# Four times twelve token blocks: 10 x 512 + 2 x 480 against 11 x 512 + 448

## The chip, the cores and the metric

The kernel runs on one core of one Trainium2 chip. The metric is the device time of one execution in microseconds (us); shown are the median of several executions and, for the profile, one execution recorded by the hardware profiler.

## The reference

Channel attention, followed by a feed-forward layer with a squared ReLU, all in float32. There are B = 4 batches of N = 6080 tokens with C = 256 channels.

```python
qn = q / (np.linalg.norm(q, axis=1, keepdims=True) + 1e-06)
kn = k / (np.linalg.norm(k, axis=1, keepdims=True) + 1e-06)
s = kn.transpose(0, 2, 1) @ qn / tau          # C x C for each batch
a = softmax(s)                                # over the last axis
x = (v @ a).reshape(B * N, C)
h = np.maximum(x @ w_in, 0.0)                 # w_in: 256 x 2048
out = h * h @ w_out                           # w_out: 2048 x 256
```

## The kernel before, in words

The softmax matrix is folded into the first weight: for each batch W = a @ w_in is made once, so a token block needs two products, v @ W with its squared ReLU, and the product with w_out. Each float32 operand is split into a high and a low part in a rounded format (called fp32r in the rows), and each product is the sum of three matmuls, high-high, high-low and low-high.

The tokens of a batch are cut into `NB` = 12 blocks (lines 75 to 78). `T` = 512 is the widest. Lines 76 and 77 give ten blocks of 512 and divide what is left, 960, into two of 480.

The first two blocks of batch 0 are worked plainly, with 512-column matmuls (`first_product`, `eight_products`). All other blocks are worked as `groups` (line 959): four groups for each block, one for every 512 of the 2048 hidden channels, 46 x 4 = 184 groups. In a group, both products are done by a seven-product scheme for 2 x 2 blocks. For it a token block is cut into two halves of `half_of(k)` columns: 256 for a block of 512, 240 for one of 480. Every matmul of a group has a 128 x 128 stationary operand of its own and `half` moving columns.

```python
987  def product(k, ps, form, block, start=False):
990      half = half_of(k)
992      for p in range(2):
994          w_hi, w_lo = (WF[k, late, i][:, p, at, :] for i in range(2))
995          for i, (wt, vt) in enumerate(((w_hi, v_hi), (w_hi, v_lo), (w_lo, v_hi))):
996              tensor.matmul(ps[:, p, :half], wt, vt[:, block, :], ...)
```

That is six matmuls for a product, and seven products for a group: 42. The second half of the work, `to_output` (lines 1031 to 1049), has 42 more in all but six early groups of batch 0 (`window_A`: three windows of 6, `window_S`: four of 6). A group is thus 84 matmuls.

The order of the work is written out by hand in `PERIOD` (lines 1268 to 1319) and kept on each engine (`InProgramOrder`). A period k issues the products of group k and, beside them, the later steps of groups k - 1 and k - 2:

```python
1269  (0, first_B),       1273  (0, copy_C),
1281  (0, second_C),      1293  (0, third_C),
1298  (0, add_C),         1305  (1, window_A1),
1308  (0, fourth_C),      1312  (1, lambda k: lo_S(k, "S1")),
```

`copy_C` is a ScalarE copy from one PSUM bank to another, onto which `second_C` adds. `add_C` is a VectorE addition with ReLU that reads what `third_C` has summed, before `fourth_C` adds to it. ScalarE squares, copies and makes the high parts; VectorE adds and makes the low parts (`A_lo`, `s_lo`, `v_lo`). SP's queue loads v (`load_v_blocks`) and the forms of W (`load_forms`, 1.8 MB for a group whatever the block's width); POOL's queue sums and stores the outputs (`combine`). In the rows the tiles ps_b, ps_h and ps_c take the products, ps_o the second half, v_hi and v_lo are the parts of v, wf the forms of W, and A, s, wo and wS the parts of the second half.

At the named points of a period (the strings "act", "dve", "sq", "pe", "norms", "mid") pieces of the next batch's attention are issued: `Gram` (12 extra matmuls in a period), the norms (`ps_n`, eight matmuls with one column), the transposes (`ps_t`) and the next weights (`ps_w`, six matmuls of 512 columns). They are counted by periods and not by tokens.

The last group of all is finished without the next period's matmuls beside it (lines 1469 to 1538): its last parts go into ps_end, two VectorE additions make end_o from it, and SP's queue stores that.

Of the kernel before, what the change touches and what calls it, by code (L numbers as in the profile page):

```python
# [32 lines left out]
def kernel(  # L33
# [27 lines left out]
    B, N, C = q.shape  # L61
# [3 lines left out]
    T = 512  # L65
# [7 lines left out]


    NB = -(-N // T)
    left = N - T * max(NB - 2, 0)
    sizes = [T] * (NB - 2) + [left // 2, left - left // 2]
    blocks = [(sum(sizes[:i]), n) for i, n in enumerate(sizes)]
    SPB = NB * NF

# [1488 lines left out]
```

## Time and profile before

| | |
|---|---|
| median of 3 runs | 2097.33 us (2096.82 to 2097.7) |
| the profiled execution's own time | 2098.59 us |
| its span, first to last instruction | 2096.8 us |
| matmuls, each with a weight load | 17158 |
| TensorE busy | 2091.1 us |
| VectorE, ScalarE busy | 1903.4 us, 1890.6 us |
| moved by DMA | 549.78 MB, 262 GB/s on average |

The profiled execution's time is 1.8 us above its span. A busy TensorE is no proof that it works at its peak, because matmuls are pipelined and a record overlaps the next one's. What counts for it is the time from one matmul's start to the next one's start: a stretch's length divided by the matmuls begun in it.

### The profile page before, as it was taken

The page shows a single profiled execution, that of the slowest core. Times are in us where ns is not written, and L with a number is a line of the kernel's source. Part 1 is how long each engine was busy: PE and PEld are TensorE (multiplying, and loading weights), DVE is VectorE, ACT ScalarE, POOL GpSimd, SP SyncE. Part 2 cuts the span into 40 slices and gives each one's busy share as a digit, 9 for nine tenths or more (in the row PEclk, how much of TensorE's full clock was granted, in tenths as well). Part 3 has the DMA queues.
Part 4 walks back from the last instruction along what each step waited for, and adds up shares of the span by engine and source line. Part 5 has one row for each costly group of instructions (what it writes and reads, how often), then busy time and mean ns, then how long its engine had stood idle before and what let it go on. Part 6 is the DMA issues. An engine that isn't in the chain of part 4 may idle for free.

```text
span 2096.8 us, 43463 instructions
## 1 busy us (share of the span) xinstructions
PE 2091.1 (100%) x17158; PEld 2053.8 (98%) x17158; DVE 1903.4 (91%) x2195; ACT 1890.6 (90%) x2379; POOL 350.1 (17%) x430
## 2 busy tenths in 40 slices
PE   9999999999999999999999999999999999999999
PEld 8789999999999999999999999999999999999999
DVE  7898999989999999989998999998999888888887
ACT  5888999889999999989999999998988998998987
POOL 0000111211122111111122111211121121121112
PEclk9999999999999999999999999999999999999999
DMA  9777888789999888789999988877999788787785
GB/s 358 222 224 269 258 255 258 235 261 307 306 279 305 267 262 251 239 243 290 295 294 282 314 252 264 249 244 249 290 284 302 229 244 253 230 248 246 233 245 152
DMA packets 258012, 549.78 MB, mean 262 GB/s; under 512 B 26672, under 2 KB 113072, under 8 KB 257808
## 3 DMA queue, kind: packets, MB, share of 16 engines
q1 hardware_dynamic: 201456, 469.02, 65.7%
q0 software_dynamic: 56352, 77.98, 18.4%
q8 instruction: 135, 2.21, 0.4%
q14 instruction: 69, 0.57, 0.1%
HBM read 433.59 MB, written 58.72 MB: 235 GB/s over the span
## 4 chain that ended last, share of the span: by engine, by line
PE 99%; ACT 1%; DVE 0%; DMA 0%; issue 0%; SPq 0%; DVEq 0%
PE ps_o L29 44%; PE ps_c L29 18%; PE ps_h L29 14%; PE ps_b L29 12%; PE gram L29 7%; PE ps_w L29 2%; ACT x L29 0%; PE ps_end L29 0%; DVE dec L29 0%; DMA qk<-in_q 0%; PE ps_n L29 0%; ACT v_hi L29 0%; ACT s L29 0%; ACT g_hi L29 0%; PE ps_t L29 0%
## 5 line engine op out<-in xcount | busy, mean ns | idle before, releaser
L29 DVE TENSOR_TENSOR x<-x 128x1024 f32<-128x1024 f32 (+2 forms) x549 | 465.3, 848 | 11.1
L29 PE MATMUL ps_c<-v_hi,wf 128*128 128x256 f32 (+1 forms) x2208 | 473.9, 278 | 0.2 <-DVE x L29 0.2
L29 POOL DMA_DIRECT2D o<-o x225 | 232.7, 1188 | 1397.4 <-ACT o L29 899.7
L29 DVE TENSOR_TENSOR s_lo<-x,s_hi 128x1024 fp32r<-128x1024 f32 (+1 forms) x366 | 441.7, 1208 | 16.9 <-ACT s_hi L29 16.5
L29 ACT ACTIVATE x<-x 128x1536 f32<-128x1536 f32 (+4 forms) x384 | 405.0, 1055 | 31.5 <-DVE x L29 29.5
L29 ACT CAST s_hi<-x 128x1024 fp32r<-128x1024 f32 (+1 forms) x366 | 381.8, 1043 | 43.1 <-DVE x L29 42.0
L29 DVE TENSOR_TENSOR A_lo<-x,A_hi 128x1536 fp32r<-128x1536 f32 (+2 forms) x183 | 313.6, 1714 | 81.6 <-ACT A_hi L29 65.3
L29 PEld LDWEIGHTS ps_c<-v_hi,wf 128*128 128x128 f32 x2208 | 375.5, 188 | 1.0 <-DVE x L29 0.4
L29 PE MATMUL ps_h<-v_hi,wf 128*128 128x256 f32 (+1 forms) x1472 | 315.9, 278 | 0.2 <-ACT x L29 0.2
L29 PE MATMUL ps_b<-v_hi,wf 128*128 128x256 f32 (+1 forms) x1472 | 315.8, 278 | 0.0
L29 PE MATMUL ps_c<-v_lo,wf 128*128 128x256 f32 (+1 forms) x1104 | 307.3, 278 | 0.0
L29 ACT CAST A_hi<-x 128x1536 fp32r<-128x1536 f32 (+2 forms) x183 | 264.8, 1447 | 0.0
L29 PEld LDWEIGHTS ps_h<-v_hi,wf 128*128 128x128 f32 x1472 | 250.4, 188 | 0.6 <-ACT x L29 0.6
L29 PEld LDWEIGHTS ps_b<-v_hi,wf 128*128 128x128 f32 x1472 | 250.3, 188 | 0.1
L29 PEld LDWEIGHTS ps_c<-v_lo,wf 128*128 128x128 f32 x1104 | 207.7, 188 | 0.1
L29 PE MATMUL ps_h<-v_lo,wf 128*128 128x256 f32 (+1 forms) x736 | 204.9, 278 | 0.0
L29 PE MATMUL ps_b<-v_lo,wf 128*128 128x256 f32 (+1 forms) x736 | 204.8, 278 | 0.0
L29 PE MATMUL ps_o<-A_hi,wo_hi 128*128 128x256 f32 (+1 forms) x897 | 192.8, 279 | 0.0
L29 PE MATMUL ps_o<-A_hi,wo_lo 128*128 128x256 f32 (+1 forms) x897 | 192.1, 278 | 0.0
L29 PE MATMUL ps_o<-A_lo,wo_hi 128*128 128x256 f32 (+1 forms) x897 | 191.8, 278 | 0.0
L29 PE MATMUL ps_o<-s_hi,wS_lo 128*128 128x256 f32 (+1 forms) x549 | 153.3, 279 | 0.0
L29 PE MATMUL ps_o<-s_lo,wS_hi 128*128 128x256 f32 (+1 forms) x549 | 153.1, 279 | 0.0
(172 smaller groups left out, 5148.9 us busy)
## 6 DMA issues: line engine op xcount, KB each, us to landing
wf<-wf_kept SPq DMA_DIRECT2D x368, 512.0 KB, 5.1
wf<-wf_kept SPq DMA_DIRECT2D x368, 384.0 KB, 4.9
o<-o POOLq DMA_DIRECT2D x114, 256.0 KB, 6.0
qk<-in_k SPq DMA_DIRECT2D x88, 256.0 KB, 5.3
qk<-in_q SPq DMA_DIRECT2D x88, 256.0 KB, 5.4
v<-in_vT SPq DMA_DIRECT2D x76, 256.0 KB, 4.8
out_T<-o POOLq DMA_DIRECT2D x152, 128.0 KB, 5.0
wf_kept<-wS SPq DMA_DIRECT2D x64, 256.0 KB, 6.1
```

The source lines that it names most:

```text
L29: return lambda *args, **kwargs: self.tc.keep_in_program_order(issue(*args, **kwargs))
```

## The change

The twelve blocks of a batch are cut in another way: eleven blocks of 512 tokens and one of 448. `NB`, the groups, the periods and all else stay as they are. Blocks 0 to 9 of each batch are as before; block 10 has 512 tokens (halves of 256 columns) and block 11 has 448 (halves of 224).

```diff
     NB = -(-N // T)
-    left = N - T * max(NB - 2, 0)
-    sizes = [T] * (NB - 2) + [left // 2, left - left // 2]
+    left = N - T * (NB - 1)
+    sizes = [T] * (NB - 1) + [left]
     blocks = [(sum(sizes[:i]), n) for i, n in enumerate(sizes)]
```

No instruction moves on any engine: each has as many rows as before, in the same order. What differs is the widths. On TensorE, at the first period of block 11 in batch 0, the first products of that block stand behind the second half of block 10. Before:

```order
L29 MATMUL ps_o_10_0_6217<-A_hi_6428,wo_hi 128x240 x2
L29 MATMUL ps_o_10_0_6217<-A_hi_6428,wo_lo 128x240 x2
L29 MATMUL ps_o_10_0_6217<-A_lo_6429,wo_hi 128x240 x2
L29 MATMUL ps_b_6532<-v_hi_11_6327,wf_0_0_6299 128x240
L29 MATMUL ps_b_6532<-v_lo_11_6328,wf_0_0_6299 128x240
L29 MATMUL ps_b_6532<-v_hi_11_6327,wf_0_1_6301 128x240
```

And in the changed kernel, at the same place:

```order
L29 MATMUL ps_o_10_0_6217<-A_hi_6428,wo_hi 128x256 x2
L29 MATMUL ps_o_10_0_6217<-A_hi_6428,wo_lo 128x256 x2
L29 MATMUL ps_o_10_0_6217<-A_lo_6429,wo_hi 128x256 x2
L29 MATMUL ps_b_6532<-v_hi_11_6327,wf_0_0_6299 128x224
L29 MATMUL ps_b_6532<-v_lo_11_6328,wf_0_0_6299 128x224
L29 MATMUL ps_b_6532<-v_hi_11_6327,wf_0_1_6301 128x224
```

Nothing has moved; the second half of block 10 is wider, the products of block 11 are narrower.

## Rows read from the trace of the kernel before

**Rows 1.** The page, part 1 and part 2: busy time, and TensorE's clock in 40 slices.
```profile
PE 2091.1 (100%) x17158; PEld 2053.8 (98%) x17158; DVE 1903.4 (91%) x2195; ACT 1890.6 (90%) x2379; POOL 350.1 (17%) x430
...
PEclk9999999999999999999999999999999999999999
```

**Rows 2.** The page, part 4: the chain that ended last, by engine.
```profile
PE 99%; ACT 1%; DVE 0%; DMA 0%; issue 0%; SPq 0%; DVEq 0%
```

**Rows 3.** The waits of PE, whole span: us in total, times, longest.
```profile
PE ps_first L29 <- DVE exp_bias L29: 1.1, 1, 1.1
PE gram L29 <- DMA qk<-in_q: 0.2, 1, 0.2
PE ps_w L29 <- ACT x L29: 0.2, 1, 0.2
PE ps_h L29 <- ACT x L29: 0.2, 1, 0.2
PE ps_c L29 <- DVE x L29: 0.2, 1, 0.2
```

**Rows 4.** The table of stretches, batch 3: blocks of 512, then of 480.
```profile
core 0: us, PE busy (x) PEld busy (x) DVE busy (x) ACT busy (x) POOL busy (x), PEclk, DMA share, GB/s
1969.40:2008.60 39.20, 39.20 (x339) 39.20 (x338) 34.56 (x38) 35.37 (x45) 7.42 (x9) 1.00 0.80 242
2027.77:2065.45 37.68, 37.68 (x339) 37.68 (x337) 32.03 (x35) 33.58 (x45) 7.57 (x10) 1.00 0.85 246
```

**Rows 5.** Timeline at the norms, PEld, then PE: start us, us, instruction.
```profile
399.52 0.75 PEld L29 LDWEIGHTS ps_n<-ones,acc 128*128 128x128 f32 x6
400.19 0.19 PEld L29 LDWEIGHTS ps_o<-A_hi,wS_hi 128*128 128x128 f32 x1
400.30 0.19 PEld L29 LDWEIGHTS ps_o<-A_hi,wo_hi 128*128 128x128 f32 x1
...
400.21 0.36 PE L29 MATMUL ps_o<-A_hi,wS_hi 128*128 128x256 f32 x1
400.42 0.28 PE L29 MATMUL ps_o<-A_hi,wo_hi 128*128 128x256 f32 x1
```

**Rows 6.** Groups of PE by shape: busy us, mean ns, idle before.
```profile
L29 PE MATMUL ps_c<-v_hi,wf 128*128 128x256 f32 x1824 | 393.7, 279 | 0.0
...
L29 PE MATMUL ps_c<-v_hi,wf 128*128 128x240 f32 x384 | 80.2, 274 | 0.2 <-DVE x L29 0.2
```

**Rows 7.** Timeline at the transposes, PEld.
```profile
429.04 0.46 PEld L29 LDWEIGHTS ps_t<-ident,s 128*128 128x128 f32 x4
429.47 0.30 PEld L29 LDWEIGHTS ps_o<-A_hi,wo_hi 128*128 128x128 f32 x2
```

**Rows 8.** Groups of DVE by shape.
```profile
L29 DVE TENSOR_TENSOR s_lo<-x,s_hi 128x1024 fp32r<-128x1024 f32 x304 | 370.2, 1220 | 12.8 <-ACT s_hi L29 12.6
...
L29 DVE TENSOR_TENSOR s_lo<-x,s_hi 128x960 fp32r<-128x960 f32 x62 | 71.5, 1153 | 4.1 <-ACT s_hi L29 4.0
```

**Rows 9.** Stretches: block 10 in batch 0, 11 in 1, first periods of block 10.
```profile
507.94:550.22 42.28, 42.28 (x357) 41.48 (x355) 38.96 (x46) 38.27 (x51) 8.49 (x11) 1.00 0.99 318
...
1064.80:1102.47 37.67, 37.67 (x338) 37.67 (x337) 34.89 (x42) 34.86 (x47) 6.29 (x7) 1.00 0.98 303
...
1023.92:1033.66 9.74, 9.74 (x86) 9.69 (x85) 7.07 (x8) 8.62 (x12) 0.00 (x0) 1.00 0.94 363
1538.38:1548.01 9.63, 9.63 (x86) 9.63 (x85) 7.32 (x9) 8.67 (x13) 0.00 (x0) 1.00 0.94 367
```

**Rows 10.** The chain that ended last, its end: start us, us, what.
```profile
2081.22 0.67 DVE x L29
2081.89 0.04 issue
2081.93 0.94 PE ps_c L29 x6
2082.87 4.84 PE ps_o L29 x42
2087.71 5.41 PE ps_end L29 x48
2093.12 0.02 issue
2093.15 0.41 DVE end_o L29
```

**Rows 11.** Stretches of 256 columns: batch 0 (two), batch 1, batch 2.
```profile
173.92:197.24 23.32, 23.32 (x200) 23.32 (x199) 22.74 (x41) 20.81 (x29) 0.00 (x0) 1.00 0.59 211
...
290.58:335.81 45.23, 45.23 (x387) 45.23 (x386) 44.55 (x48) 43.31 (x54) 7.42 (x9) 1.00 0.83 265
...
677.29:722.09 44.80, 44.80 (x386) 44.80 (x385) 43.37 (x46) 42.87 (x53) 8.50 (x11) 1.00 0.87 282
...
1191.85:1236.65 44.80, 44.80 (x386) 44.80 (x385) 43.36 (x46) 42.86 (x53) 7.46 (x9) 1.00 0.83 259
```

## Prediction

> **What bounds the kernel now.** I read the page's busy lines first. TensorE is busy for the whole span and its weight loads for 98% of it, at a clock of 2.4 GHz from end to end [rows 1]; the chain that ended last is 99% TensorE [rows 2], and its own waits in the whole program are five, 1.9 us together [rows 3]. So almost nothing but the number of matmuls and the time from one matmul's start to the next can move the end. VectorE at 91% and ScalarE at 90% are the next limits, but they are not what ends the time.
>
> The second view is the table of stretches [rows 4]. Both stretches are four periods of batch 3, a period being one group of four hidden-channel blocks with 84 matmuls, so 336 starts each (the count also holds matmuls that overlap an edge). With 256 columns they take 39.20 us, 116.67 ns a matmul; with 240 columns 37.68 us, 112.14 ns. Columns fell by 6.25%, time by 3.9%. If spacing followed columns, 240 would stand at 116.67 x 240/256 = 109.4 ns. It does not: something else already holds the 240-column stream.
>
> The third view says what. In the norms, eight products have one output column, so no streaming time to speak of [rows 5]. Their weight loads still start 112 ns apart: from 399.52 to 400.19 us are six spacings, 111.7 ns each, and the next load, of a weight in the same format as the main products use, is again followed after 0.11 us. The first wide matmul behind them is shown with 0.36 us instead of 0.28, because it waits for its weights. A weight load of 128 columns thus needs about 111.7 ns whatever streams beside it, and each matmul here has its own load. At 256 columns the stream is the longer of the two; at 240 the load is, and the remaining 0.4 ns looks like jitter between them. The mean record falls only from 279 to 274 ns [rows 6], and that too contains the wait for weights.
>
> **The change, part by part.** It moves no instruction. Per batch, block 10 goes from 480 to 512 tokens and block 11 from 480 to 448, so a half goes from 240 to 256 and from 240 to 224 columns. Number of matmuls, weight loads, form loads and periods stay.
>
> 1. *Block 10, 240 to 256 columns.* Four batches x four periods x 84 = 1344 matmuls, each (116.67 - 112.14) = 4.53 ns longer [rows 4]: **+6.1 us**. All of it lies on the path.
> 2. *Block 11, 240 to 224 columns.* Again 1344 matmuls. No row has 224 columns in this format. The upper bound is no gain: they stay at 112.14 ns [rows 4]. The nearest row below is the load alone, 111.7 ns [rows 5]; I take it, because every cause of the extra 0.4 ns gets weaker with a shorter stream: 1344 x 0.47 = **-0.6 us**. Two lower prices stay as ends: 110 ns, the smallest spacing that a row shows for such a load (two loads in 0.30 us, less 0.19 for the last) [rows 7], which is -2.9 us; and plain proportion to columns, 116.67 x 224/256 = 102.1 ns, -13.5 us.
>    The Trainium skill, "TensorE: Matmul & The Clock Gate", section "LDWEIGHTS (loading the stationary operand)", gives a load as its columns divided by 1.2, so 106.7 ns for 128. The six loads of [rows 5] took 111.7 each, and I go by them; by the page's price this term would be 1344 x 5.4 = -7.3 us and the sum below would turn to about -1.3 us, an estimate from that page.
> 3. *VectorE and ScalarE.* Their operations follow columns with a fixed part: 1.220 us for 1024 elements, 1.153 for 960 [rows 8]. In block 11 they get shorter while TensorE keeps its pace, so slack grows: in batch 1 VectorE had 34.89 of 37.67 us there [rows 9]. In block 10 they grow by at most 5.8%: in batch 0, with the next weights formed beside it, VectorE goes from 38.96 to at most 41.2 us, and the stretch from 42.28 to 43.8 [rows 9]. The cover stays; cost 0. If it went, the next thing late would be ScalarE's `copy_C`, onto whose result `second_C` adds.
> 4. *The step from wide to narrow.* At the first narrow period the other engines still handle wide blocks of the two periods before, while TensorE already runs faster. That cost once: block 10's first period in batch 1 took 9.74 us, in batch 2 9.63 [rows 9], with the 0.2 us wait for VectorE of [rows 3]. The same step now stands one block later at the same TensorE pace. Between -0.1 and +0.1 for each of four batches; I take 0.
> 5. *Transfers.* The loads of v for these blocks, their partial sums and their stores change size by a fifteenth; the loads of the weight forms, most of the bytes, do not. TensorE's one wait for a DMA is at the start [rows 3]. 0.
> 6. *The end.* The last group is 224 instead of 240 wide. The 42 and 48 matmuls there run at 115 and 113 ns [rows 10] and keep their loads. What shrinks is the VectorE addition before the last ps_c (0.67 us) and the last sum (0.41), by a fifteenth less the fixed part, some 0.03 each, and the last store a little: **-0.1 us**, between 0 and -0.2.
>
> Sum: 6.1 - 0.6 - 0.1 = **+5.4 us**. The profiled execution took 2098.59 us (a span of 2096.8 and 1.8 around it), so it would take 2104.0. The median of the three runs, 2097.33, lies 1.26 below that execution; on it the forecast is **2102.7 us**.
>
> **The rivals.** (a) *The load is no floor; spacing keeps falling with columns* (the other side). Its place is block 11 alone. Then item 2 is -13.5, the sum 6.1 - 13.5 - 0.1 = -7.5, and the time 2089.8. It decides from where 224 columns come below 107.6 ns: there 1344 x 4.5 pays for item 1. Against it: 240 columns miss proportion by 2.8 ns already [rows 4], and one column still takes 112 [rows 5].
>
> (b) *The load is a floor, but a lower one.* For it: the transposes' four loads take 0.46 us, with 0.14 for the last, so 107 ns apart [rows 7]. Then item 2 is 1344 x 5.1 = -6.9, the sum -0.9, the time 2096.4: no difference. Against it: these loads are of another kind (their records are 0.14 long, those of the main products 0.19). The skill's 106.7 ns speaks for this case, as said under item 2.
>
> (c) *The wide stream behind the narrow one settles in a slower rhythm.* In batch 0 the same 256-column stream took 45.23 us for 384 matmuls, 117.8 ns each, in batch 1 44.80, 116.67 [rows 11], with no wait in either; and it had that rhythm from 173.92 us on (23.32 us for 198). If the new 224-to-256 step locked it in, batch 3 would pay 1.1 ns for each of 84 matmuls in 38 periods up to its narrow block, 3.6 us, and batches 1 and 2 for 96 in some 24 periods up to the norms, 2.5 us each: 2105.2 to 2106.3 for one of them, 2111.3 for all. Against it: after all three 240-to-256 steps the stream ran at 116.67 (batch 1 and 2 in [rows 11], batch 3 in [rows 4]), and after the load-bound norms of [rows 5] too.
>
> **How the numbers follow.** The forecast's mechanism has 0.72, (c) 0.12, (b) 0.11, (a) 0.05. The low end of the range takes the 110 ns load: 6.1 - 2.9 - 0.1 = +3.1, 2100.4. The high end takes no gain in block 11 and (c) in batch 3: 6.1 + 3.6 - 0.2 = +9.5, 2106.8. That leaves out (a), most of (b) and the worst of (c), under 0.2. What a measurement here can tell from no change is about 0.2%, 4.2 us, so slower begins at 2101.5: the forecast, less a little at its low edge, and (c), 0.80; the same is (b) and that edge, 0.15; faster is (a), 0.05.
>
> **What would show it.** In batch 3, four periods with 256 columns should go on taking 39.2 us, block 10's among them, and four with 224 columns 37.5 (load bound), against 37.7 with 240. If block 11 takes 36.0 or 34.3, (b) or (a) is right, and the prediction fails there. The records of 224-column matmuls should stay near 274 ns, since they hold a wait for weights. A 256-column stretch after a narrow block at 117.8 would be (c). The waits of TensorE should stay within some us; a new one on VectorE or ScalarE near the start of block 11 would be item 4.

## The result, and the profile after

The changed kernel takes 2111.51 us (median of 4 runs, 2110.89 to 2112.94) against 2097.07 for the kernel before beside it: a ratio of 1.0071, with a 95% interval of 1.0058 to 1.0083. It is slower, as forecast, but by 14.4 us and not by 5.4, and outside the range. The profiled execution took 2111.87 us, its span is 2110.1.

The page's first part and the waits of PE, of the changed kernel (to set beside [rows 1, 3]):

```profile
PE 2104.7 (100%) x17158; PEld 2067.7 (98%) x17158; DVE 1906.0 (90%) x2195; ACT 1891.7 (90%) x2379; POOL 349.8 (17%) x430
```
```profile
PE ps_first L29 <- DVE exp_bias L29: 1.1, 1, 1.1
PE ps_w L29 <- ACT x L29: 0.2, 1, 0.2
PE ps_h L29 <- ACT x L29: 0.2, 1, 0.2
```

TensorE is busy 13.6 us longer with as many matmuls, and waits for nobody more than before. So the time went into the spacing of matmuls (the time from one start to the next). The table of stretches of the changed kernel tells where (first the stretch, then its length and the engines' busy time with their counts):

```profile
529.60:539.40 9.80, 9.80 (x87) 9.80 (x85) 9.07 (x13) 9.00 (x12) 1.19 (x1) 1.00 0.96 265
569.72:588.48 18.76, 18.76 (x171) 18.76 (x169) 17.92 (x24) 16.73 (x23) 4.52 (x5) 1.00 1.04 308
678.49:723.72 45.23, 45.23 (x387) 45.23 (x385) 43.52 (x46) 42.91 (x53) 8.49 (x11) 1.00 0.86 278
1196.87:1242.09 45.22, 45.22 (x386) 45.22 (x385) 43.51 (x46) 42.88 (x53) 7.45 (x9) 1.00 0.80 261
1822.54:1862.11 39.57, 39.57 (x338) 39.57 (x337) 34.74 (x38) 35.47 (x45) 7.40 (x9) 1.00 0.78 232
2020.40:2059.98 39.58, 39.58 (x339) 39.58 (x338) 34.52 (x39) 35.28 (x45) 5.16 (x5) 1.00 0.76 221
```

Each stretch runs from the first matmul of a period to that of another. The first is a period of block 10 in batch 0: 84 matmuls in 9.80 us, 116.67 ns each. The second is two periods of block 11, 168 matmuls at 111.67 ns. Both are what the prediction took. The next three lie in blocks that the change does not touch, in batches 1, 2 and 3: 117.8 ns for each of 384, 384 and 336 matmuls, where the same columns before ran at 116.67 [rows 4, 11]. The last is block 10 of batch 3, at 117.8 as well.

Period by period against the trace before, those untouched wide periods give back 2.53 us in batch 1 (24 periods, up to the norms), 2.53 in batch 2 and 3.55 in batch 3 (38 periods): 8.6 us. Blocks 10 and 11 of the four batches give 5.6, of which 0.4 is the slower spacing again, in batch 3's block 10, and the shorter end is taken off. That is 14.2; the spans differ by 13.3, because this execution also reached the first group 0.65 us sooner, ahead of anything that the change touches, and its periods beside the norms were 0.3 us shorter.

The groups of TensorE by shape in the changed kernel (compare [rows 6]) and the chain at its end (compare [rows 10]):

```profile
L29 PE MATMUL ps_c<-v_hi,wf 128*128 128x256 f32 x2016 | 437.7, 280 | 0.0
...
L29 PE MATMUL ps_c<-v_hi,wf 128*128 128x224 f32 x192 | 39.9, 274 | 0.1
```
```profile
2094.81 0.63 DVE x L29
2095.44 0.04 issue
2095.49 0.93 PE ps_c L29 x6
2096.41 4.70 PE ps_o L29 x42
2101.11 5.37 PE ps_end L29 x48
```

A 224-column record lasts 274 ns like a 240-column one, as it should if it contains the wait for its weights; the 42 and 48 matmuls of the end went from 115.2 and 112.7 ns to 111.9 and 111.9.

### The profile page after: what moved, and what is told of

It reads as the page before. It is cut to its first block, busy times and chain, and to the rows that moved or that the text cites. A ratio compares the mean times of both kernels' runs of the same rounds, so it can differ in the third digit from the quotient of the medians.

```text
span 2110.1 us, 43463 instructions
## 1 busy us (share of the span) xinstructions
PE 2104.7 (100%) x17158; PEld 2067.7 (98%) x17158; DVE 1906.0 (90%) x2195; ACT 1891.7 (90%) x2379; POOL 349.8 (17%) x430
## 4 chain that ended last, share of the span: by engine, by line
PE 99%; ACT 0%; DVE 0%; issue 0%; DVEq 0%
PE ps_o L29 45%; PE ps_c L29 18%; PE ps_h L29 14%; PE ps_b L29 12%; PE gram L29 7%; PE ps_w L29 2%; PE ps_end L29 0%; ACT x L29 0%; DVE dec L29 0%; PE ps_first L29 0%; PE ps_n L29 0%; ACT g_hi L29 0%; PE ps_t L29 0%; DVE g_lo L29 0%; ACT wi_hi_w L29 0%
## 5 line engine op out<-in xcount | busy, mean ns | idle before, releaser
L29 ACT COPY x<-ps_c 128x512 f32<-128x512 f32 (+1 forms) x184 | 107.3, 583 | 53.1 <-PE ps_c L29 43.5
```

The costliest lines, as they stand in the source:

```text
L29: return lambda *args, **kwargs: self.tc.keep_in_program_order(issue(*args, **kwargs))
```

## The experiments

**Bringing the faster spacing back.** The changed kernel, with one-column products ahead of the third period of batches 1, 2 and 3; the product behind them overwrites what they write, so nothing is left out.

```diff
         B2[k] = two_halves("h0", f"ps_b{k}")
+        for m in range({(1, 0, 2): 4, (2, 0, 2): 1, (3, 0, 2): 2}.get(groups[k], 0)):
+            tensor.matmul(B2[k][:, 0, m : m + 1], ones, ones[:, 0:1], start=m == 0, stop=True, skip_group_check=True)
         product(k, B2[k], A11, B11, start=True)
```

> The changed kernel with some one-column products put ahead of the first product of block 0's third period in batches 1, 2 and 3 (four, one and two of them, each of two weight loads; what they write is overwritten by the product's start). Theory 1 (the rhythm is TensorE's own: the stream of 256 columns has two stable spacings, and a stretch held by its weight loads, 224 columns, leaves it in the slower one, as one-column products bring it back to the faster one at the norms): from there on 116.67 ns a matmul instead of 117.78, at least in batch 1, which has as many loads as the norms; a period of 96 takes 11.20 us and not 11.31. If one and two products are enough as well, the time falls by 2.5, 2.5 and 3.9 us less some 1.9 for 14 loads and the pauses behind them: about 2104.5 us. Theory 2 (something outside TensorE that the new widths altered, transfers or the other engines' reading, slows every matmul): 117.78 stays, and the time rises by the added 1.9 us to 2113.4.

It took 2105.18 us (5 runs; kernel before 2097.70, ratio 1.0038, 1.0024 to 1.0053). The timeline of PE at the single product of batch 2, then stretches of batches 1, 2 and 3 behind the products:

```profile
1125.97 0.28 PE L29 MATMUL ps_b<-ones 128*128 128x1 f32 x2
1126.10 0.36 PE L29 MATMUL ps_b<-v_hi,wf 128*128 128x256 f32 x1
1126.31 0.28 PE L29 MATMUL ps_b<-v_lo,wf 128*128 128x256 f32 x1
```
```profile
632.56:677.36 44.80, 44.80 (x386) 44.80 (x385) 40.22 (x43) 42.86 (x53) 9.11 (x11) 1.00 1.04 313
1148.60:1193.40 44.80, 44.80 (x387) 44.80 (x385) 40.23 (x43) 42.84 (x53) 9.14 (x11) 1.00 1.03 313
1659.12:1698.32 39.20, 39.20 (x339) 39.20 (x337) 34.67 (x38) 35.45 (x45) 7.40 (x9) 1.00 0.81 242
```

The first wide matmul behind the product is 0.36 us long, with a gap of 0.21 to the next; from there on it is 116.67 ns (44.80/384, 39.20/336) in all three batches, two weight loads being enough, and it stays so up to the next narrow block. Blocks, loads, widths and the other engines' work are the same as in the changed kernel, so theory 2 has fallen: the spacing is carried by TensorE's own stream. The time came to 0.7 us of theory 1's.

Theory 1 also says that the norms bring the faster spacing back, and that does not hold. They too have eight one-column matmuls and the same matmul of 0.36 us behind them. Two stretches of the changed kernel in batch 1, the first from just behind the norms up to the product `ps_b<-diag,ones`, before which TensorE's stream pauses for 0.3 us, the second behind that product:

```profile
878.78:887.02 8.24, 8.24 (x71) 8.24 (x71) 7.72 (x23) 7.05 (x12) 1.19 (x1) 1.00 1.01 315
887.99:907.36 19.37, 19.37 (x169) 19.37 (x167) 18.23 (x23) 17.27 (x25) 4.39 (x6) 1.00 0.85 263
```

Behind the norms the stream kept 117.7 ns (8.24 us for 70 matmuls), in batch 2 as well; only behind the next pause was it 116.7 (19.37 for 166). In batch 0 the norms did end the slower spacing, in both kernels. And the same two stretches of the kernel before, in batch 1, go the other way:

```profile
875.70:883.87 8.17, 8.17 (x71) 8.17 (x71) 7.65 (x23) 7.05 (x12) 1.19 (x1) 1.00 1.01 318
884.86:904.41 19.55, 19.55 (x168) 19.55 (x167) 18.40 (x23) 17.44 (x26) 4.41 (x6) 1.00 0.87 266
```

There the same pause and product took the stream from 116.7 ns to 117.8, up to the transposes. So an interruption can change the spacing either way or leave it; the added products brought the faster one back in all three places here, and nothing shows what decides.

**The widths without a wide stream behind them.** 512 + 448 in batch 3 alone (the lines that read `blocks` now do so by batch and block; they are left out here):

```diff
-    sizes = [T] * (NB - 1) + [left]
-    blocks = [(sum(sizes[:i]), n) for i, n in enumerate(sizes)]
+    sizes = [[T] * 10 + pair for pair in ([480, 480],) * 3 + ([512, 448],)]
+    blocks = {(b, i): (sum(sizes[b][:i]), n) for b in range(B) for i, n in enumerate(sizes[b])}
```

> 512 + 448 in batch 3 alone; batches 0 to 2 keep 480 + 480. There is then no wide stream behind a narrow block of 224 columns. Theory 1: batch 3 stays at 116.67 ns up to block 11 and pays the direct terms alone, four periods of 84 at +4.5 ns and four at -0.5, and the shorter end: +1.5 - 0.15 - 0.25 = +1.1 us against the kernel before, about 2098.2 us. Theory 2, or a slower rhythm that comes with 224 columns or with this program wherever they stand: 117.8 in batch 3, +3.6 more, 2101.8 us.

It took 2098.67 us (10 runs; before 2097.70, ratio 1.0004, 0.9994 to 1.0013): +1.0 us, where 1.1 was worked out, though the interval holds no change too. Batch 3, block 9, block 10, and one period of block 11:

```profile
1967.00:2006.20 39.20, 39.20 (x338) 39.20 (x337) 34.67 (x38) 35.45 (x45) 7.41 (x9) 1.00 0.81 242
2006.20:2045.40 39.20, 39.20 (x338) 39.20 (x337) 34.44 (x39) 35.24 (x45) 5.16 (x5) 1.00 0.76 225
2064.51:2073.89 9.38, 9.38 (x87) 9.38 (x85) 7.10 (x9) 7.18 (x11) 1.19 (x1) 1.00 0.71 175
```

Block 10 is at 116.67 ns here, at 117.8 in the changed kernel: what lies behind a narrow block decides, not the program's having one.

**The width of the narrow block.** The same edit with other pairs in each batch (`[496, 464], [488, 472], [504, 456], [512, 448]`):

> A pair of widths for each batch: 496 + 464 in batch 0, 488 + 472 in batch 1, 504 + 456 in batch 2, 512 + 448 in batch 3, so halves of 248 and 232, 244 and 236, 252 and 228, 256 and 224 columns. If spacing is the larger of the load's 111.7 ns and 0.4557 ns a column: 232, 236, 228 and 224 at 111.7 (four periods of 84 without other work: 37.5 us), 244 a little over 111.7, 248 at 113.0, 252 at 114.8. Theory 1 says that 228 and 232, held by the load, leave the next batch's stream at 117.78; 236 is open, since 240 does not. All three steps slow: about 2108 us; none: about 2099.5. If the load were no floor, 232 would be at 105.7 and 228 at 103.9.

It took 2100.80 us (8 runs; before 2097.70, ratio 1.0012, 1.0002 to 1.0022), so nearer to "none" than to "all three". Stretches of 248, 232, 236 and 228 columns, then 256 behind the last three:

```profile
528.86:538.51 9.65, 9.65 (x86) 9.65 (x85) 8.77 (x13) 8.66 (x12) 1.19 (x1) 1.00 0.99 279
568.50:587.27 18.77, 18.77 (x171) 18.77 (x169) 18.23 (x23) 17.11 (x24) 4.51 (x5) 1.00 1.07 305
1083.19:1102.00 18.81, 18.81 (x170) 18.81 (x169) 18.39 (x23) 17.29 (x24) 4.51 (x5) 1.00 1.06 309
1598.83:1617.59 18.76, 18.76 (x170) 18.76 (x169) 18.10 (x23) 16.91 (x24) 4.10 (x6) 1.00 1.00 266
654.20:699.00 44.80, 44.80 (x387) 44.80 (x385) 42.67 (x45) 42.87 (x53) 7.36 (x9) 1.00 0.95 291
1146.57:1191.36 44.79, 44.79 (x386) 44.79 (x385) 40.03 (x43) 42.83 (x53) 8.01 (x10) 1.00 0.99 288
1656.54:1695.74 39.20, 39.20 (x339) 39.20 (x337) 34.66 (x38) 35.44 (x45) 7.40 (x9) 1.00 0.80 242
```

Two things. The load's floor holds: 168 matmuls take 18.76 us at 228 columns, 18.77 at 232, 18.81 at 236, that is 111.7, 111.7 and 112.0 ns. And 248 columns take 114.9 ns, more than the columns' share of 116.67 (113.0); 244 take about 113.5 and 252 about 116.0 to 116.5, also more than expected. But 228 and 232 columns, as much held by their loads as 224, left the next batch at 116.67. So theory 1 was right on TensorE and wrong on what makes the step: not any load-bound stretch does it.

**Nearly equal blocks**, 508 and 504 (`[[508] * 8 + [504] * 4] * B`):

> All blocks nearly equal: eight of 508 and four of 504 in each batch, so halves of 254 and 252 columns and no stretch that its weight loads hold. If spacing follows columns above the load's 111.7 ns: 115.75 and 114.84 ns a matmul, in a batch 8 x 115.75 + 4 x 114.84 = 1385.4 in place of 10 x 116.67 + 2 x 112.14 = 1391.0, and 5.6 ns x 336 x 4 = 7.5 us less than before: about 2089.6 us. Rival: these widths have a slower rhythm of their own (as 240 does, 2.8 ns above its columns' share), with 117 ns or so: 2100 us or more.

It took 2127.46 us (4 runs; before 2097.70, ratio 1.0141, 1.0125 to 1.0156), the rival and worse. Stretches of 254 and of 252 columns, batch 3, and a new wait of PE:

```profile
1719.41:1759.03 39.62, 39.62 (x338) 39.62 (x337) 34.61 (x38) 35.25 (x45) 6.86 (x9) 1.00 0.79 232
1996.69:2035.78 39.09, 39.09 (x338) 39.09 (x337) 34.30 (x38) 34.98 (x45) 7.41 (x9) 1.00 0.79 242
```
```profile
PE ps_b L29 <- DMA wf<-wf_kept: 4.3, 4, 1.5
```

That is 117.9 ns for 254 columns and 116.3 for 252: with 254 columns, more time than 256 at its best. From 240 (112.1 ns) over 248 (114.9) to 254 the spacing climbs, but not by width alone. In the run on widths near 224, below, 254 and 250 columns stood at 117.1 and 116.9 ns (95 matmuls each):

```profile
1041.12:1052.24 11.12, 11.12 (x97) 11.12 (x96) 10.90 (x15) 10.79 (x14) 3.01 (x3) 1.00 0.91 278
1557.02:1568.13 11.11, 11.11 (x98) 11.11 (x96) 10.62 (x15) 10.65 (x14) 3.00 (x3) 1.00 0.88 257
```

So 250 columns took longer there than 252 here, and 254 has more than one spacing too. In a batch 8 x 117.9 + 4 x 116.3 is 17.4 ns more than the 1391.0 before, so spacing adds 17.4 x 336 x 4 = 23.4 us. About 4 us more are waits for weight forms. Behind each of the two places where TensorE waited, the granted clock fell to 0.50 (1.2 GHz) for some us: from 642 to 645 us, for one, matmuls started 213 ns apart, which lost about 1.5 us each time. Together that is 30.7 us, near the 29.8 measured.

**The place of the narrow block.** 448 as block 10, 2, 8 and 3 of batches 0 to 3 (`[T] * at + [448] + [T] * (11 - at)`):

> The block of 448 at another place in each batch: block 10 in batch 0, 2 in batch 1, 8 in batch 2, 3 in batch 3; all other blocks have 512. Theory A (a step from 224 to 256 columns leaves the stream in the slower rhythm wherever it stands, until one-column products or a pause bring it back): 117.8 ns behind each of the four, in batch 3 for all 30 periods up to the end. The direct terms give 4 x 1.4 = 5.4 us, the rhythm some 0.8 + 1.2 + 0.3 + 2.8 = 5.1: about 2108 us. Theory B (it comes from the step into a new batch, with the next batch's Gram products mixed in): at most the one behind batch 0, and 2103.7 us.

It took 2107.82 us (2 runs; before 2096.78, ratio 1.0051, 1.0033 to 1.0070), 2108 having been worked out for theory A. Batch 3 ahead of the narrow block, in it, and behind it:

```profile
1699.31:1738.51 39.20, 39.20 (x338) 39.20 (x337) 34.42 (x39) 35.18 (x45) 7.40 (x9) 1.00 0.80 244
1757.64:1776.40 18.76, 18.76 (x171) 18.76 (x169) 15.61 (x19) 15.84 (x22) 5.62 (x7) 1.00 0.95 276
1795.75:1835.32 39.57, 39.57 (x338) 39.57 (x337) 34.74 (x38) 35.48 (x45) 7.37 (x9) 1.00 0.78 235
```

116.67 ns, 111.67, 117.8, and no Gram products in any of them. The slower rhythm stands behind all four places (in batch 1 the stream had it already, from batch 0, so three steps count); behind the one in batch 2 it ended after two periods, beside products of 512 columns. Theory B has fallen.

**Widths near 224.** Pairs of 512 + 448, 508 + 452, 500 + 460, 480 + 480:

> Last pairs of 512 + 448, 508 + 452, 500 + 460 and 480 + 480 in batches 0 to 3: the narrow halves are 224, 226, 230 and 240, the wide ones 256, 254, 250 and 240. The run with 228, 232 and 236 left the next batch at 116.67. Theory A: 224 leaves batch 1 at 117.78, 230 leaves batch 3 at 116.67, and 226 (batch 2) tells whether the bound lies between 224 and 226 or between 226 and 228. If any block held by its loads did it at random, batches 2 and 3 could be slow too. Direct terms 1.4 + 1.7 + 1.0 = 4.1 us, and 2.5 for each slow batch 1 or 2: 2104 us with one, 2106.5 with both.

It took 2104.26 us (4 runs; before 2096.78, ratio 1.0035, 1.0020 to 1.0049), the sum for one slow batch. The wide stretches behind 224, 226 and 230:

```profile
609.30:654.53 45.23, 45.23 (x387) 45.23 (x385) 39.42 (x41) 42.90 (x53) 10.94 (x13) 1.00 0.98 286
...
1127.81:1172.61 44.80, 44.80 (x387) 44.80 (x385) 39.41 (x41) 42.71 (x53) 10.93 (x13) 1.00 1.01 296
...
1640.89:1680.09 39.20, 39.20 (x338) 39.20 (x337) 34.66 (x38) 35.33 (x45) 7.40 (x9) 1.00 0.80 238
```

224 leaves 117.8, 226 leaves 116.67, and so does 230.

**The slower rhythm in batch 0.** The kernel before, with the reset of the first experiment (one product) at two periods, `{(0, 2, 2): 1, (0, 5, 1): 1}`:

> The kernel before (480 + 480), with one one-column product (two loads) ahead of the first product of batch 0's third period (block 2) and of its period 13 (block 5). In its profile the periods of batch 0 from the third to the twentieth run at 117.78 ns. Theory 1 (such products bring the faster rhythm back): 116.67 from there on, 0.1 us less in each of some 18 periods, 1.8 us, less 0.4 for the products and pauses: 1.4 us under the kernel before in executions that were slow there, nothing or +0.4 in those that were fast there anyway. Rival (in batch 0 something else holds the stream at 117.78): +0.4 us.

It took 2097.55 us (11 runs; before 2096.78, 17 runs; ratio 1.0003, 0.9994 to 1.0012): no difference that can be told. Its profile, ahead of the second product and behind it:

```profile
232.58:242.83 10.25, 10.25 (x90) 10.25 (x89) 10.17 (x13) 9.84 (x15) 4.36 (x6) 1.00 1.01 297
312.56:357.36 44.80, 44.80 (x387) 44.80 (x385) 43.57 (x46) 42.85 (x53) 7.41 (x9) 1.00 0.84 259
```

Behind the second product it is 116.67 ns (44.80/384); a period between the two had gone back to the slower spacing (87 matmuls in 10.25 us, 117.8 ns), behind a short pause of the stream. So the products do bring the faster one back here too, but not for good: the pause that ended it, 0.26 us long, is another that turned a fast stream slow. The profiles of the second, third, fifth and sixth experiments had the faster rhythm at the start of batch 0 without any help, so there was little to gain. No version beat the kernel before.

**Below 224.** Batches of thirteen blocks, the last of 444, 440 and 432 (`[256, 260, 444], [260, 260, 440], [264, 264, 432], [480, 480]` behind ten of 512):

> Batches of thirteen blocks, so that the last can be narrower than 448: ten of 512 and 256, 260, 444 in batch 0, 260, 260, 440 in batch 1, 264, 264, 432 in batch 2, and 512s, 480, 480 in batch 3. The last halves are 222, 220 and 216 columns, and the blocks behind them have 256. If every width at or under 224 leaves the slower rhythm: batches 1, 2 and 3 start at 117.78. If 224 alone does it: all three at 116.67. The time itself says nothing here: three batches have four more groups of 84 matmuls, which the weight loads hold at 111.7 ns, 9.4 us each, 12 x 9.4 = 113 us more, about 2212 us with 2.5 to 3.6 more for each slow batch.

The time, 2219.24 us (2 runs), says nothing here. The wide stretches behind 222, 220 and 216 columns, the waits, and the clock behind one of them:

```profile
677.66:722.89 45.23, 45.23 (x386) 45.23 (x385) 43.53 (x46) 42.90 (x53) 7.42 (x9) 1.00 0.82 257
...
1218.99:1263.79 44.80, 44.80 (x387) 44.80 (x385) 43.55 (x46) 42.69 (x53) 7.44 (x9) 1.00 0.82 255
...
1756.48:1795.68 39.20, 39.20 (x338) 39.20 (x337) 34.66 (x38) 35.43 (x45) 7.44 (x9) 1.00 0.77 235
```
```profile
PE ps_b L29 <- DMA wf<-wf_kept: 4.6, 4, 1.7
```
```profile
636.00:638.00 2.00, 2.00 (x12) 2.00 (x10) 0.00 (x0) 1.89 (x3) 0.00 (x0) 0.50 1.05 420
```

222 leaves 117.8, but between its block and the wide stretch lie such waits and some us at a granted clock of 0.50, so this step is not a clean one; 220 and 216 leave 116.67. So no threshold was found: of the widths tried, 224 does it each time that the stream ahead was fast (all three steps of the changed kernel, three of the four places, and batch 1 of the run on widths near it), 222 once, and 216, 220, 226, 228, 230, 232, 236 and 240 do not. All but 240 of these others rest on one step each.

This run also settles the price of a load, since its extra blocks are much narrower. Four periods of 132 columns:

```profile
1662.07:1699.59 37.52, 37.52 (x338) 37.52 (x338) 20.99 (x37) 21.30 (x45) 7.49 (x10) 1.00 0.80 238
```

That is 111.67 ns for each of 336 matmuls, as with 224 columns.

## Why the prediction was wrong, and where it was right

- *What bounds it, and item 1.* Right. Block 10 went to 116.67 ns in batches 0 to 2, +4.53 ns for each matmul.
- *Item 2.* Right to the digit: 224 columns run at 111.67 ns, the price of the load read at the norms [rows 5]. Rivals (a) and (b) have fallen with it; 132 and 228 columns stand there too, 226, 230 and 232 within 0.1 ns. The Trainium skill's page "TensorE: Matmul & The Clock Gate", section "LDWEIGHTS (loading the stationary operand)", gives a load as its columns divided by 1.2, which is 106.7 ns for 128; these stretches disagree by 5 ns.
- *Items 3 to 6.* Right in their cost: no new wait on VectorE, ScalarE or a DMA. Two reasons were wrong. The one stall that item 4 put down to the step to narrower columns, in block 10's first period of batch 1, stayed there (9.93 us, against 9.80 in batch 2), though that block is now wide, so it did not come from the step. The end shrank by 0.26 us, where 0.1 was taken, and 0.18 of it came from the 42 and 48 matmuls that item 6 left as they were.
- *The step that failed.* The sum has no term for the wide blocks that the change does not touch: it took them at 116.67 ns behind block 11, as before. They ran at 117.8 up to the norms of batches 1 and 2 and through batch 3: 8.6 us, and 0.4 more in batch 3's block 10. This was rival (c), whose mechanism and price were right, 2111.3 us for all three batches against a measured 2111.5; that the totals agree so closely is in part luck, since (c) left out that 0.4, and the kernel before beside it took 0.3 us less than the 2097.33 that it was added to. I gave it 0.12, on the ground that the stream had come back to 116.67 after all three 240-to-256 steps and after the load-bound norms. The first holds but was another case: the step from 224 differs from the one from 240. The second holds for some 70 matmuls only: behind the next pause the trace before shows batch 1 at 117.8 again (884.86 to 904.41 us, above), a row that would have warned that the spacing can change with no change of width. The rows gave two rhythms for one width, with nothing that said what chose between them; three steps of another width were worth far less than the 0.88 I set against (c). The range took the case in for one batch and left out that all three would do the same, though they are the same step.
- *The high end.* With (c) in all batches and no gain in block 11 it would have been 2111.8 and held the result.

Why 224 and not 226 or 220 stays open. That the rhythm is carried by TensorE's stream is shown, since products that only interrupt it changed it for most of three batches; what decides which of the two follows an interruption or a step is not. A guess that some widths leave loads and streams in another phase to each other was not tested by anything that would show phase, and each reading of a step is from one profiled execution of its kernel.

## What to carry to other kernels

Where each matmul has its own weight load, price a narrower one as the larger of load and stream, and read the load's price from a stretch with next to no columns. Just below 256 columns fewer columns can cost more, so widths there are measured and not interpolated. If a trace shows two spacings for the same shape with no wait, find out what sets them before changing what stands ahead: 1% over the rest of a batch outweighed the whole edit here.

## What the runs showed of the hardware that was not expected

The same stream of 256-column matmuls, each with a 128-column load, at 2.4 GHz throughout, has two stable spacings, 116.67 and 117.8 ns, and keeps either for hundreds of us. Two, four or eight one-column matmuls and the pause behind them moved it to the faster one in all four places where the stream was slow; the eight of the norms did not in batches 1 and 2 of the changed kernel (117.7 ns behind them), and a pause of 0.33 us in the kernel before moved it from 116.7 to 117.8. A load of 128 columns held the stream at 111.67 ns with 132 moving columns as with 224. And 254 columns were slower than 256 at its best, by 1.2 ns a matmul in one run (117.9 against 116.67) and by 0.4 in another (117.1).
